# Two layers of long convolution and MLP on one core: another element order in the products with v, and the shift filter loaded once and copied on chip

## The chip, the core and the metric

The kernel runs on one core of one Trainium2 chip. Such a core has five engines, each with its own instruction stream: TensorE (PE; its weight loads are listed apart as PEld), VectorE (DVE), ScalarE (ACT), GpSimd (POOL) and SyncE (SP), which here only issues DMAs. Matmul results go to PSUM, from which DVE or ACT must fetch them; everything else lies in SBUF, 128 partitions wide. The metric is the device time of one execution in microseconds (us); the profile shows one execution, its times counted from the start of its span.

## The reference, cut to what matters

```python
def _A_ref(q, k, v, shift_k, ssm_k, ssm_D):            # B = 1, S = 2048, D = 512
    ks = shift_k.shape[-1]                             # 4 taps
    k_pad = jnp.pad(k, ((0, 0), (ks - 1, 0), (0, 0)))
    k_shift = jnp.zeros_like(k)
    for t in range(ks):
        k_shift = k_shift + k_pad[:, t:t + S, :] * shift_k[:, ks - 1 - t][None, None, :]
    kv = k_shift * v
    ...
    y = y + kv * ssm_D[None, None, :]                  # y: kv convolved with ssm_k over S, by FFT
    return q * y

def _B_ref(x, w1, b1, w2, b2):                         # F = 1376
    y = _layernorm(x, axis=-1)
    h = _gelu(jnp.einsum("bsd,df->bsf", y, w1) + b1)
    return jnp.einsum("bsf,fd->bsd", h, w2) + b2

x = A_q
x = x + _A_ref(_layernorm(x, axis=-1), A_k, A_v, A_shift_k, A_ssm_k, A_ssm_D)
x = x + _B_ref(_layernorm(x, axis=-1), B_w1, B_b1, B_w2, B_b2)
x = x + _A_ref(...)                                    # the same once more
x = x + _B_ref(...)
return x
```

All inputs and the output are bf16. The change touches `k_shift` (a filter of four taps over time, one for each channel) and `kv = k_shift * v`.

## The kernel before, in words

k, v and the filters are the same in both layers, so the long convolution `y` is computed once, in the first part of the program, and both layers use it. That part is a two-stage Fourier transform made of matmuls; the rest of the program, from some 96 us on, is nearly all MLP matmuls on PE.

The first part is not scheduled by a compiler. Each piece of work is an item with a name (`plan.add`), and the text table `ORDER` (line 19) lists all items with an engine letter: `kvm00.D` puts item kvm00 on DVE, `.A` is ACT, `.G` POOL, `.S` SP, and `.P2` is PE with PSUM buffer 2. Every engine runs its items strictly in the order of that table, and waits at an item until its inputs are there. There are four PSUM buffers, 4 KB a partition each, so two PSUM banks of 2 KB; an item that writes one waits until the last reader of that buffer is through.

The names that matter here:

- `lF, lK.., lk0, lk1, lW, lb1, lx0, lv0, lv1, lH`: loads issued by SP (line 279, the four of `ssm_k` line 342): a Fourier table, `ssm_k`, k, the table `Wt`, a bias, part of q, v in two halves, and a last table. They stand in one DMA queue.
- `lT0` to `lT3`: the shift filter, loaded four times (line 349), each time to 32 partitions. `taps_t` is a zeroed tile of 128 partitions x 16 groups x 7 columns, and load `lTi` puts the four taps of 16 channel groups into columns i to i+3 of partitions 32i to 32i+31. In memory a channel's four taps are 8 bytes, and in the tile they land 14 bytes apart, so each load is 512 pieces of 8 bytes.
- `dg0` to `dg3` (line 409, POOL): multiply the taps by a 32 x 32 identity, which gives banded matrices `DG`; they wait for all four `lT`.
- `kT0` to `kT3`: k transposed on PE and copied to SBUF.
- `kv00` to `kv31` (PE, lines 474 and 475): the shift as matmuls of transposed k with `DG`. Item `kv{cc}{o}` makes, for channels cc modulo 4 and half o of the token blocks, 1024 fp32 values a partition in one PSUM buffer.
- `kvm00` to `kvm31` (DVE, line 483): the products, in place in `uv`, which holds v as bf16, 16 token blocks x 512 channels a partition. There are eight; each waits for its `kv` and for its half of v.
- `U{cc}S{q}` (PE, line 303): the first Fourier stage of the products, evicted to the tiles `ZT` by ACT or DVE (lines 211 and 213); then `U..T` (transposes), `X` (line 507), `T` (products with the filter's spectrum, line 522), `V` (line 530) and so on.
- `kd` (lines 366 and 367, evicted at 211 and 213): four small corrections to the loaded `ssm_k`; each eviction writes 32 bf16 a partition, 64 elements apart in SBUF.
- `s00`, `s01`, `s02`: layer norm of a part of q on DVE, POOL and DVE; `sa`, `sb`: copies inside SBUF by DMA; `lM`: a 2 MB table that takes the place of transposed k and so waits for all `kv`.

In PSUM a product's buffer is ordered e (4), i (8 token blocks), c (32); in `uv` the same element lies at token block i, channel 16 c + 4 e + cc.

Of the kernel before, what the change touches and what calls it, by code (L numbers as in the profile page):

```python
# [103 lines left out]
def kernel(ctx: ExitStack, tc: tile.TileContext, A_q, A_k, A_v, A_shift_k, A_ssm_k, A_ssm_D,  # L104
                 B_x, B_w1, B_b1, B_w2, B_b2, out):
    nc = tc.nc
    P = 128
    _, S, D = A_q.shape
    F = B_w1.shape[1]
    KS = A_shift_k.shape[1]  # L110
# [54 lines left out]
    taps_t = const.tile([P, NG4, NU], BF16, name="taps_t")  # L165
# [108 lines left out]
    with tc.tile_pool(name="ps", bufs=1, space=bass.MemoryType.PSUM) as ps:  # L274
        pf = [ps.tile([P, 1024], F32, name=f"p{i}") for i in range(4)]
        plan = _Plan({"ps": 4, "xb": NXB, "zt": NZT})

        def load(name, dst, src, nbytes, deps=(), eng="S", rank=0):
            return plan.add(name, {eng: 400}, deps, lambda it: nc.sync.dma_start(dst, src), dma=("copy", nbytes), rank=rank)  # L279
# [16 lines left out]
        def first_stage(name, src, cs, dst, deps, xbar, edeps):  # L296
# [22 lines left out]
            for h in range(2):  # L319
# [9 lines left out]
                def mms(o, h=h):  # L329
# [8 lines left out]
        kd4 = k_d.rearrange(TOK, p=P)  # L338
# [17 lines left out]
        lW = load("lW", Wt[:], W_h.ap().bitcast(BF16), 2 ** 20)  # L356
        lH = load("lH", GPt[:], GP_h.ap().bitcast(BF16), 2 ** 16)
# [3 lines left out]
        for c in range(16):  # L361
# [8 lines left out]
            def mms(o, c=c):  # L370
                for m in range(8):
                    for r in range(2):
                        nc.tensor.matmul(o[64 * r:64 * r + 64, m, :], Kd[:, 8 * c + m, :], Ft[:, 256 + P * r:256 + P * r + P],  # L373
                                         start=True, stop=True)
            _, e = mm_evac(f"KS{c // 2}{c % 2}", KSC, [kd, lF], mms, [8, P],
                           lambda c=c: Zk.rearrange("p k (g m) -> p k g m", g=4)[:, :, :, 8 * c:8 * c + 8],
                           src=lambda v: v.rearrange("p m (g k) -> p k g m", g=4))
            KSe.append(e)
        KW, KX, KWp = [], [], []
        for j in range(NA // 2):  # L380
            def mms(o, j=j):
                for i in range(2):
                    nc.tensor.matmul(o[:, i, :], Wt[:, 2 * j + i, :], Zk[:, 2 * j + i, :], start=True, stop=True)
            pe, ev = mm_evac(f"K2{j}", K2C, [lW] + KSe, mms, [2, D], lambda j=j: ZK[:, :, 2 * j:2 * j + 2, :],
                             src=lambda v: v.rearrange("p k (t c) -> p t k c", t=CT))
# [14 lines left out]
        for i, (n, c) in enumerate(((13, 11), (1, 1), (1, 1))):  # L400
            it = plan.add(f"wm{i}", {"P": 427 * c}, [], warm, take=["ps"])
            it["n"] = n
            it["free"] = [(it, "ps")]
        kTp, kTe, dg = [], [], []
        DG = [view(xbb[NXB - CT + ct], [4, NU * 32]) for ct in range(CT)]
        for ct in range(CT):
            def diag(it, ct=ct):
                eng = nc.vector if it["eng"] == "D" else nc.gpsimd
                eng.tensor_tensor(DG[ct].rearrange("p g (u c) -> p g u c", c=32),
                                  apf(ID4, 0, [[32, P], [0, 4], [0, NU], [1, 32]]),  # L410
                                  apf(taps_t, ct * NU, [[NG4 * NU, P], [CT * NU, 4], [1, NU], [0, 32]]), ALU.mult)
            dg.append(plan.add(f"dg{ct}", {"D": 1000, "G": 2000}, lT, diag))
        for q in range(4):
            def mms(o, q=q):
                for g in range(NG4):
# [1 line left out]
            pe, ev = mm_evac(f"kT{q}", 1250, [lk[q // 2]], mms, [NG4, P], lambda q=q: kT[:, :, q, 2:2 + P], True)  # L417
# [9 lines left out]
        lx0 = load("lx0", lna0, xd[:, 0:GT, :], 2 ** 19)  # L427
# [39 lines left out]
        def taps(cc, o, deps):  # L467
            def mms(v):
                for e in range(4):
                    for b in range(2):  # L470
                        g, q = CT * e + cc, 2 * o + b
                        before = kT[:, g, q - 1, 2:2 + P] if q else kT[:, g, 3, 1:1 + P]
                        d = v[:, 2 * e + b, :]
                        nc.tensor.matmul(d, kT[:, g, q, 2:2 + P], DG[cc][:, e, 0:P], start=True, stop=False)
                        nc.tensor.matmul(d[:, 0:96], before, DG[cc][:, e, P:NU * 32], start=False, stop=True)  # L475
            pe = plan.add(f"kv{cc}{o}", {"P": 800}, deps + [dg[cc]],
                          lambda it: mms(view(pf[it["slot"]["ps"]], [8, P])), take=["ps"])
            kvp.append(pe)

            def mul(it):  # L480
                us = uv[:, 8 * o:8 * o + 8, :].rearrange("p i (c e x) -> p i c e x", e=4, x=4)[:, :, :, :, cc]
                ks = view(pf[pe["slot"]["ps"]], [4, 8, 32]).rearrange("p e i c -> p i c e")
                nc.vector.tensor_tensor(us, ks, us, ALU.mult)  # L483
            return plan.add(f"kvm{cc}{o}", {"D": 1150}, [pe, lv[o]], mul, free=[(pe, "ps")])
        um = [[taps(cc, o, [kTe[2 * o], kTe[2 * o + 1], kTe[2 * o - 1]]) for o in range(2)] for cc in range(CT)]
# [59 lines left out]
        w1 = load("w1", W1t[:], B_w1.rearrange("(ct p) f -> p ct f", p=P), 1376 << 10, Vps[0] + Vps[1])  # L545
# [284 lines left out]
```

## Time and profile before

| | |
|---|---|
| median of the timed runs (3) | 256.64 us, from 256.40 to 256.84 |
| the profiled execution | 255.45 us, of which the span is 253.6 us |
| mean granted TensorE clock | 0.991 |
| busy in the span: PE, DVE, ACT, POOL | 234.0, 178.3, 140.1, 37.6 us |
| DVE's products (line 483) | 32.7 to 51.3 us, 8 instructions |
| first MLP matmuls (line 662) | 95.7 us |

The profile's rows are read so. A row of a timeline has the start, the length, the engine, the line of the kernel, the operation, what it writes and reads, the shape a partition count x elements, and how many instructions were merged into the row; in brackets the idle time of the engine ahead of it and what ended that. A row of a group has the count, the busy time and the mean duration of one in ns, and behind the second bar the idle time ahead of such instructions. Names of tiles are those of the program; `arena` stands for several regions of one large tile (k, v, spectra and weights among them), `p` for the PSUM buffers. Durations of neighbours on an engine can overlap by some 0.1 to 0.2 us, since the next one starts while the last ends.

### The profile page before, as it was taken

How to read it: one execution, taken by the hardware profiler on the slowest of the kernel's cores; microseconds unless marked ns; L12 is line 12 of the kernel's file. 1: busy time of each engine (PE TensorE's matmuls, PEld its weight loads, DVE VectorE, ACT ScalarE, POOL GpSimd, SP SyncE). 2: the span in 40 equal slices, each digit the busy share in tenths (PEclk: the TensorE clock that was granted, in tenths of full speed). 3: DMA queues.
4: the chain of work that ended last, by engine and by line, in shares of the span. 5: the costliest groups of instructions: out<-in, count | busy, mean ns of one | idle time of the engine just before them, and what ended most of it. 6: DMA issues, size and time to landing. Idle time of an engine off the chain costs nothing.

```text
span 253.6 us, 4775 instructions
## 1 busy us (share of the span) xinstructions
PE 234.0 (92%) x1941; PEld 140.1 (55%) x1941; DVE 178.3 (70%) x316; ACT 140.1 (55%) x197; POOL 37.6 (15%) x49
## 2 busy tenths in 40 slices
PE   6967978789599899999999999999999999999994
PEld 2755657688498749744444444444444444444443
DVE  0585999989999989889889897866866862022022
ACT  2576975779679999933703713713713713713700
POOL 5000480016500031310111110110110110000000
PEclk9999997999999999999999999999999999999999
DMA  7999988299966999440510404004006006001001
GB/s 134 180 277 325 345 301 301 60 361 203 257 101 130 163 263 187 145 83 0 44 42 1 83 0 85 0 0 84 3 26 141 0 23 145 0 27 56 3 28 55
DMA packets 58129, 29.55 MB, mean 117 GB/s; under 512 B 50582, under 2 KB 54395, under 8 KB 57212
## 3 DMA queue, kind: packets, MB, share of 16 engines
q1 hardware_dynamic: 58100, 29.25, 48.3%
q8 instruction: 15, 0.25, 0.4%
q14 instruction: 6, 0.05, 0.1%
q10 hardware_dynamic: 8, 0.00, 0.0%
HBM read 15.10 MB, written 2.10 MB: 68 GB/s over the span
## 4 chain that ended last, share of the span: by engine, by line
PE 66%; DMA 12%; DVE 10%; SPq 5%; ACT 4%; issue 2%; DVEq 0%; ACTq 0%
PE po L752 30%; PE ph L718 26%; DMA arena<-in_A_v_dram 4%; DVE arena L483 4%; DMA arena<-arena 4%; PE p L662 4%; SPq L342 4%; DMA Wt<-tabW 3%; DVE arena L522 3%; PE p L530 2%; ACT ZT L211 2%; SPq L279 2%; PE p L507 1%; ACT xb L211 1%; ACT arena L211 1%
## 5 line engine op out<-in xcount | busy, mean ns | idle before, releaser
L720 ACT ACTIVATE arena<-ph,B 128x512 bf16<-128x512 f32 (+1 forms) x77 | 52.9, 687 | 78.4 <-PE ph L718 78.3
L752 PE MATMUL po<-arena 128*128 128x512 bf16 (+2 forms) x363 | 77.4, 372 | 0.0
L718 PE MATMUL ph<-arena 128*128 128x512 bf16 (+1 forms) x308 | 67.6, 379 | 0.0
L752 PEld LDWEIGHTS <-arena 128*128 128x128 bf16 (+1 forms) x363 | 35.4, 98 | 40.5
L757 DVE TENSOR_TENSOR arena<-po,arena 128x512 bf16<-128x512 f32 (+1 forms) x33 | 21.6, 673 | 46.4 <-PE po L752 46.4
L718 PEld LDWEIGHTS <-arena 128*128 128x128 bf16 (+1 forms) x308 | 30.8, 100 | 35.9
L211 ACT ACTIVATE arena<-p 128x1024 bf16<-128x1024 f32 (+7 forms) x45 | 39.8, 983 | 13.6 <-PE p L373 5.7
L211 ACT ACTIVATE ZT<-p 128x1024 bf16<-128x1024 f32 (+1 forms) x25 | 24.1, 1026 | 7.5 <-PE p L303 7.4
L213 DVE CAST arena<-p 128x1024 bf16<-128x1024 f32 (+1 forms) x13 | 13.2, 1077 | 11.1 <-PE p L367 9.0
L233 DVE BATCH_NORM_STATS2 lstm<-arena 128x6 f32<-128x512 bf16 x32 | 20.1, 681 | 0.3
L522 DVE TENSOR_TENSOR arena<-xb,arena 128x2048 bf16<-128x2048 bf16 (+1 forms) x15 | 20.1, 1404 | 0.0
L233 DVE BATCH_NORM_STATS2 lstg<-arena 128x6 f32<-128x512 bf16 x32 | 19.7, 677 | 0.0
L530 PE MATMUL p<-arena,arena 128*128 128x128 bf16 x256 | 16.2, 219 | 3.7 <-DVE arena L213 3.5
L483 DVE TENSOR_TENSOR arena<-p,arena 128x1024 bf16<-128x1024 f32 x8 | 18.6, 2502 | 0.4 <-PE p L475 0.4
L249 POOL TENSOR_TENSOR lrsm<-lrsm,mhalf 128x4 f32<-128x4 f32 (+2 forms) x11 | 9.9, 903 | 55.9 <-DVE lrsm L243 55.9
L249 POOL TENSOR_TENSOR lrsg<-lrsg,mhalf 128x4 f32<-128x4 f32 x8 | 8.1, 1016 | 65.9 <-DVE lrsg L246 65.8
L530 PEld LDWEIGHTS <-arena 128*128 128x128 bf16 x256 | 14.8, 98 | 4.7 <-DVE arena L522 3.4
L254 DVE TENSOR_SCALAR arena<-arena,lmvg,lrsg 128x512 bf16<-128x512 bf16 x32 | 11.0, 408 | 6.8 <-POOL lrsg L249 6.8
L211 ACT ACTIVATE xb<-p 128x1024 bf16<-128x1024 f32 x15 | 15.0, 1063 | 0.0
L254 DVE TENSOR_SCALAR arena<-arena,lmvm,lrsm 128x512 bf16<-128x512 bf16 x32 | 11.5, 415 | 2.4 <-POOL lrsm L249 2.4
L303 PE MATMUL p<-Ft,arena 128*128 128x256 bf16 x64 | 10.0, 291 | 3.1 <-DVE arena L483 3.0
L213 DVE COPY arena<-p 128x2048 bf16<-128x2048 bf16 x9 | 10.7, 1218 | 2.8 <-PE p L416 1.7
(69 smaller groups left out, 217.0 us busy)
## 6 DMA issues: line engine op xcount, KB each, us to landing
arena<-arena SPq DMA_DIRECT2D x8, 512.0 KB, 4.4
arena<-in_A_ssm_k_dram SPq DMA_DIRECT2D x4, 512.0 KB, 7.2
arena<-in_A_k_dram SPq DMA_DIRECT2D x2, 1024.0 KB, 9.6
arena<-in_A_v_dram SPq DMA_DIRECT2D x2, 1024.0 KB, 8.5
arena<-tabM SPq DMA_DIRECT2D x1, 2048.0 KB, 8.3
out_dram<-arena SPq DMA_DIRECT2D x15, 128.0 KB, 1.7
arena<-in_A_q_dram SPq DMA_DIRECT2D x1, 1536.0 KB, 7.0
arena<-in_B_w_dram SPq DMA_DIRECT2D x1, 1376.0 KB
```

The costliest lines, as they stand in the source:

```text
L211: nc.scalar.activation(dst, src, AF.Copy)
L213: nc.vector.tensor_copy(dst, src)
L233: nc.vector.bn_stats(self.st[:, i, 0, :], x_t[:, GT * g + i, :] if src is None else src[:, i, :])
L249: nc.gpsimd.tensor_tensor(self.rs[:, a:b], self.rs[:, a:b], mhalf[:, a:b], ALU.pow)
L254: eng.tensor_scalar(out=dst[:, i, :], in0=xs, scalar1=self.mv[:, i, 0:1], scalar2=self.rs[:, i:i + 1], op0=ALU.subtract, op1=ALU.mult)
L483: nc.vector.tensor_tensor(us, ks, us, ALU.mult)
L522: eng.tensor_tensor(kk, x2, kk, ALU.mult)
L530: nc.tensor.matmul(o[:, i, :], spec[:, cc, ka + i, :], Mt[:, ka + i, r, :], start=r == 0, stop=r == 1)
L718: nc.tensor.matmul(o.rearrange("p (i t) -> p i t", t=P), W1t[:, ct, ft * P:ft * P + m], lt[:, a:b, ct, :], start=ct == 0, stop=ct == CT - 1)
L720: nc.scalar.activation(hT[0:m, ft, a * P:b * P], o, AF.Gelu_apprx_tanh, bias=B1[0:m, ft:ft + 1])
L752: nc.tensor.matmul(po[:, a:b], hT[0:m, ft, i * P:(i + 1) * P], W2t[0:m, ft, a:b], start=ft == 0, stop=ft == FT - 1)
L757: nc.vector.tensor_tensor(xs, po[:, a:b], xs, ALU.add)
```

## The change

Two things are edited. First, the products walk their elements in another order: before, innermost e, then c, then i; now innermost c, then i, outermost e. PSUM is then read in a row, and in `uv` an element is followed by the one 16 channels on instead of the one 4 channels on. Which elements are multiplied does not change.

Second, the four loads of the shift filter become one, `lT`, which brings the filter four times to 32 partitions each, 128 bytes a partition, into a region `raw`; a new item `tb` on POOL, ahead of `dg0`, copies it to the four places in `taps_t`. The region `raw` lies where `sa1` and `sb1` write later. In the table, four words for loads go, `lT.S` comes between `lx0` and `lk1`, and `tb.G` ahead of `dg0.G`; nothing else moves in it.

```diff
 ORDER = """
...
-lx0.S lk1.S KS41e.A lT0.S kT1.P3
+lx0.S lT.S lk1.S KS41e.A kT1.P3
...
-KS21.P1 lT3.S KS71e.D
+KS21.P1 KS71e.D
...
-K26.P1 K210e.A dg0.G
+K26.P1 K210e.A tb.G dg0.G
...
 """
...
-        lT = [load(f"lT{i}", taps_t[32 * i:32 * i + 32, :, i:i + KS],
-                   apf(A_shift_k, 0, [[NG4 * KS, 32], [KS, NG4], [1, KS]]), 2 ** 13) for i in range(4)]
+        raw = place("raw", [P, NG4, KS], 82 * K)
+        lT = load("lT", raw, apf(A_shift_k, 0, [[0, 4], [NG4 * KS, 32], [1, NG4 * KS]]), 2 ** 14)
+
+        def band(it):
+            eng = nc.vector if it["eng"] == "D" else nc.gpsimd
+            for i in range(4):
+                eng.tensor_copy(taps_t[32 * i:32 * i + 32, :, i:i + KS], raw[32 * i:32 * i + 32, :, :])
+        tb = plan.add("tb", {"D": 400, "G": 600}, [lT], band)
...
-            dg.append(plan.add(f"dg{ct}", {"D": 1000, "G": 2000}, lT, diag))
+            dg.append(plan.add(f"dg{ct}", {"D": 1000, "G": 2000}, [tb], diag))
...
             def mul(it):
-                us = uv[:, 8 * o:8 * o + 8, :].rearrange("p i (c e x) -> p i c e x", e=4, x=4)[:, :, :, :, cc]
-                ks = view(pf[pe["slot"]["ps"]], [4, 8, 32]).rearrange("p e i c -> p i c e")
+                us = uv[:, 8 * o:8 * o + 8, :].rearrange("p i (c e x) -> p e i c x", e=4, x=4)[:, :, :, :, cc]
+                ks = view(pf[pe["slot"]["ps"]], [4, 8, 32])
                 nc.vector.tensor_tensor(us, ks, us, ALU.mult)
```

SP's queue in the first part of the program, from the table `Wt` to the last table, as one piece of the difference (`taps_t` is the banded tile, `in_A_shift_k_dram` the filter, `arena_67` holds a part of q here, `arena_65` k, `arena_66` v):

```order
 L279 DMA Wt<-tabW 128x4096
 L279 DMA arena_64<-in_B_b_dram 1x1376
-L279 DMA taps_t<-in_A_shift_k_dram 32x16x4 x2
 L279 DMA arena_67<-in_A_q_dram 128x2048
+L279 DMA arena_64<-in_A_shift_k_dram 128x1x64
 L279 DMA arena_65<-in_A_k_dram 128x4096
-L279 DMA taps_t<-in_A_shift_k_dram 32x16x4 x2
 L279 DMA arena_66<-in_A_v_dram 128x4096 x2
 L279 DMA GPt<-tabGP 128x256
```

Three DMAs fewer stand ahead of v, and the filter's one load stands ahead of the second half of k.

POOL from the program's preparations to the layer norm's scale (`ID_71` is the identity, `xb_105` to `xb_108` hold the banded matrices):

```order
 L185 COPY ID_71<-IDt 32x32 x4
 L190 COPY Dz<-arena_64 1x128 x3
-L409 TENSOR_TENSOR xb_105<-ID_71,taps_t 128x896
-L409 TENSOR_TENSOR xb_108<-ID_71,taps_t 128x896
-L409 TENSOR_TENSOR xb_107<-ID_71,taps_t 128x896
-L409 TENSOR_TENSOR xb_106<-ID_71,taps_t 128x896
+L355 COPY taps_t<-arena_64 32x16x4 x4
+L415 TENSOR_TENSOR xb_105<-ID_71,taps_t 128x896
+L415 TENSOR_TENSOR xb_108<-ID_71,taps_t 128x896
+L415 TENSOR_TENSOR xb_107<-ID_71,taps_t 128x896
+L415 TENSOR_TENSOR xb_106<-ID_71,taps_t 128x896
 L246 TENSOR_SCALAR lrsg_111<-lmvg_110 128x4
```

Four copies come ahead of the four diagonals, which only change their line.

DVE at the beginning of the products, before (`arena128_67` is transposed k, `arena112_66` is `uv`, `p0` to `p3` the PSUM buffers, in brackets the semaphores waited for):

```order
L213 COPY arena128_67<-p3_127 128x16x128 [waits PE_49,Activation_49]
L213 COPY arena128_67<-p2_126 128x16x128 [waits PE_49,Activation_49]
L483 TENSOR_TENSOR arena112_66<-p1_125,arena112_66 128x1024 [waits DMAHW7_49,PE_49,Activation_49]
L483 TENSOR_TENSOR arena112_66<-p0_124,arena112_66 128x1024 [waits PE_49,Activation_49]
L483 TENSOR_TENSOR arena112_66<-p1_125,arena112_66 128x1024 [waits DMAHW0_49,PE_49]
```

And with the change:

```order
L213 COPY arena128_67<-p3_127 128x16x128 [waits PE_49,Activation_49]
L213 COPY arena128_67<-p2_126 128x16x128 [waits PE_49,Activation_49]
L489 TENSOR_TENSOR arena112_66<-p1_125,arena112_66 128x4x256 [waits DMAHW4_49,PE_49,Activation_49]
L489 TENSOR_TENSOR arena112_66<-p0_124,arena112_66 128x4x256 [waits PE_49,Activation_49]
L489 TENSOR_TENSOR arena112_66<-p1_125,arena112_66 128x4x256 [waits DMAHW5_49,PE_49]
```

The products keep their places and buffers; the shape tells the new order, four runs of 256, and the loads of v signal through other semaphores.

More of the change, by code (lines that the diff above doesn't have):

```diff
@@ L18 @@
 ORDER = """
-lF.S lK11.S wm0.P3 lK00.S kd6.P0 kd6e.D KS70.P1 KS60.P2 KS70e.A lK01.S kd0.P3 KS61.P0 kd0e.D KS00.P3 KS61e.A KS60e.D KS11.P1 KS10.P2 KS11e.A KS01.P0 lK10.S lk0.S kd2.P1 KS00e.D kd2e.A lW.S KS71.P3 KS10e.D lb1.S KS01e.A KS21.P1 lT3.S KS71e.D KS21e.A KS20.P2 KS30.P0 kd4.P3 kd4e.A lT1.S KS31.P1 KS30e.A KS20e.D KS51.P3 KS40.P2 KS31e.D KS40e.A KS41.P0 KS51e.D KS50.P1 kT0.P2 lx0.S lk1.S KS41e.A lT0.S kT1.P3 kT0e.A KS50e.D K20.P0 K211.P1 K22.P2 K20e.A K22e.A kT1e.D K28.P3 K212.P0 K211e.D K28e.D K23.P1 K212e.A K214.P2 K215.P3 K214e.D K23e.A bB.P0 K29.P1 lT2.S lv0.S lv1.S bBe.D K215e.A K25.P2 K29e.A K210.P0 kT3.P3 K25e.A s00.D K26.P1 K210e.A dg0.G kT2.P2 K26e.A K27.P0 kT3e.D K27e.A K24.P3 dg3.G kv00.P1 kT2e.D lH.S K21.P2 K24e.A sb2.S kv30.P0 dg2.G K21e.A K213.P3 kvm00.D kv01.P1 U0S0.P20 kvm30.D K213e.A kv20.P0 U3S0.P31 kvm01.D U0S0e.A dg1.G s01.G kvm20.D U3S0e.A U0S2.P1 kv21.P2 U0S1.P0 sb1.S sa2.S kv11.P3 U0S2e.A U0S1e.A U2S0.P12 kvm21.D U2S0e.A U0S3.P2 U0S3e.A kv31.P0 kvm11.D U2S3.P3 kvm31.D kv10.P1 U2S2.P2 U2S3e.A U2S2e.A U2S1.P0 kvm10.D sb3.S s02.D U2S1e.A U0T0.P3 U3S1.P1 sb0.S U3S2.P2 U0T0e.D sa0.S U2T0.P0 U2T0e.D U3S1e.A U3S3.P1 X00.P30 U3S2e.A U3S3e.A X00e.A U0T1.P2 X20.P01 sa1.S U1S0.P10 U2T1.P3 U0T1e.D X20e.A X02.P22 lM.S U2T1e.D U1S2.P0 U1S0e.A X03.P13 sa3.S U1S3.P3 X02e.A X03e.A U1S1.P2 X21.P14 U1S2e.D U1S1e.A U1S3e.D U3T0.S X21e.A X22.P05 X23.P26 X01.P37 T00.G X22e.A T03.D X01e.A T02.D V00.P1 X23e.A U1T0.P0 ly.S V03.P3 V00e.A U3T1.S T20.D V02.P2 V03e.A T01.D U1T1.P1 U1T0e.D X30.P38 V01.P0 V02e.A U1T1e.D X11.P20 X30e.A X10.P13 T22.G V01e.A X12.P32 X11e.D T23.D V20.P02 X10e.A T21.D X13.P21 V22.P1 X12e.A X13e.A V22e.A V23.P3 T10.D V20e.A V21.P2 lx.S V23e.D X31.P17 Z01.S V21e.A Z00.S V10.P00 X33.P35 X32.P26 Z21.S T11.D X31e.A T12.D Z03.S V10e.A Z20.S X32e.A wm2.P1 V11.P1 V12.P0 T13.D T30.D V11e.A V13.P2 V12e.A V30.P11 T31.D V13e.A wm1.P0 X33e.A V30e.A T32.D Z23.S Z10.S T33b.D V31.P2 Z13.S V32.P0 T33a.D Z11.S V33b.P3 V33a.P1 w1.S V32e.D V31e.A V33be.A V33ae.A TD0a.P2 TD0b.P3 TD3.P0 TD0ae.A TD0be.A Y00.P1 LG1.D Z12.S TD3e.A Y00e.A TD1.P2 Y01.P3 g00.D q1.G Y32.P0 Y01e.A g01.D Z22.S h00.D TD1e.A Z02.S h01.D p00.G b00.D p01.G Y32e.A Y30.P1 Y02.P2 Y30e.A b01.D Y12.P3 Y10.P0 LT0.P1 Y02e.A g02.D Y12e.A TD2.P2 h02.D LT1.P3 LT0e.A p02.G w3.S a1.D w2.S TD2e.A LT1e.A M0a.P1 M0b.P2 M1b.P3 Y10e.A M0ae.A b02.D g10.D M1be.A M1a.P0 M0be.A LT2.P1 h10.D Y20.P3 LT2e.A Y22.P2 w4.S M2a.P1 g12.D Y20e.A M1ae.A M2c.P3 Y22e.A M2ce.A p10.G h12.D p12.G M2ae.A M2b.P0 b12.D b10.D M2be.A LT3.S
@@ new lines @@
+lF.S lK11.S wm0.P3 lK00.S kd6.P0 kd6e.D KS70.P1 KS60.P2 KS70e.A lK01.S kd0.P3 KS61.P0 kd0e.D KS00.P3 KS61e.A KS60e.D KS11.P1 KS10.P2 KS11e.A KS01.P0 lK10.S lk0.S kd2.P1 KS00e.D kd2e.A lW.S KS71.P3 KS10e.D lb1.S KS01e.A KS21.P1 KS71e.D KS21e.A KS20.P2 KS30.P0 kd4.P3 kd4e.A KS31.P1 KS30e.A KS20e.D KS51.P3 KS40.P2 KS31e.D KS40e.A KS41.P0 KS51e.D KS50.P1 kT0.P2 lx0.S lT.S lk1.S KS41e.A kT1.P3 kT0e.A KS50e.D K20.P0 K211.P1 K22.P2 K20e.A K22e.A kT1e.D K28.P3 K212.P0 K211e.D K28e.D K23.P1 K212e.A K214.P2 K215.P3 K214e.D K23e.A bB.P0 K29.P1 lv0.S lv1.S bBe.D K215e.A K25.P2 K29e.A K210.P0 kT3.P3 K25e.A s00.D K26.P1 K210e.A tb.G dg0.G kT2.P2 K26e.A K27.P0 kT3e.D K27e.A K24.P3 dg3.G kv00.P1 kT2e.D lH.S K21.P2 K24e.A sb2.S kv30.P0 dg2.G K21e.A K213.P3 kvm00.D kv01.P1 U0S0.P20 kvm30.D K213e.A kv20.P0 U3S0.P31 kvm01.D U0S0e.A dg1.G s01.G kvm20.D U3S0e.A U0S2.P1 kv21.P2 U0S1.P0 sb1.S sa2.S kv11.P3 U0S2e.A U0S1e.A U2S0.P12 kvm21.D U2S0e.A U0S3.P2 U0S3e.A kv31.P0 kvm11.D U2S3.P3 kvm31.D kv10.P1 U2S2.P2 U2S3e.A U2S2e.A U2S1.P0 kvm10.D sb3.S s02.D U2S1e.A U0T0.P3 U3S1.P1 sb0.S U3S2.P2 U0T0e.D sa0.S U2T0.P0 U2T0e.D U3S1e.A U3S3.P1 X00.P30 U3S2e.A U3S3e.A X00e.A U0T1.P2 X20.P01 sa1.S U1S0.P10 U2T1.P3 U0T1e.D X20e.A X02.P22 lM.S U2T1e.D U1S2.P0 U1S0e.A X03.P13 sa3.S U1S3.P3 X02e.A X03e.A U1S1.P2 X21.P14 U1S2e.D U1S1e.A U1S3e.D U3T0.S X21e.A X22.P05 X23.P26 X01.P37 T00.G X22e.A T03.D X01e.A T02.D V00.P1 X23e.A U1T0.P0 ly.S V03.P3 V00e.A U3T1.S T20.D V02.P2 V03e.A T01.D U1T1.P1 U1T0e.D X30.P38 V01.P0 V02e.A U1T1e.D X11.P20 X30e.A X10.P13 T22.G V01e.A X12.P32 X11e.D T23.D V20.P02 X10e.A T21.D X13.P21 V22.P1 X12e.A X13e.A V22e.A V23.P3 T10.D V20e.A V21.P2 lx.S V23e.D X31.P17 Z01.S V21e.A Z00.S V10.P00 X33.P35 X32.P26 Z21.S T11.D X31e.A T12.D Z03.S V10e.A Z20.S X32e.A wm2.P1 V11.P1 V12.P0 T13.D T30.D V11e.A V13.P2 V12e.A V30.P11 T31.D V13e.A wm1.P0 X33e.A V30e.A T32.D Z23.S Z10.S T33b.D V31.P2 Z13.S V32.P0 T33a.D Z11.S V33b.P3 V33a.P1 w1.S V32e.D V31e.A V33be.A V33ae.A TD0a.P2 TD0b.P3 TD3.P0 TD0ae.A TD0be.A Y00.P1 LG1.D Z12.S TD3e.A Y00e.A TD1.P2 Y01.P3 g00.D q1.G Y32.P0 Y01e.A g01.D Z22.S h00.D TD1e.A Z02.S h01.D p00.G b00.D p01.G Y32e.A Y30.P1 Y02.P2 Y30e.A b01.D Y12.P3 Y10.P0 LT0.P1 Y02e.A g02.D Y12e.A TD2.P2 h02.D LT1.P3 LT0e.A p02.G w3.S a1.D w2.S TD2e.A LT1e.A M0a.P1 M0b.P2 M1b.P3 Y10e.A M0ae.A b02.D g10.D M1be.A M1a.P0 M0be.A LT2.P1 h10.D Y20.P3 LT2e.A Y22.P2 w4.S M2a.P1 g12.D Y20e.A M1ae.A M2c.P3 Y22e.A M2ce.A p10.G h12.D p12.G M2ae.A M2b.P0 b12.D b10.D M2be.A LT3.S
```

## The prediction

> **What bounds the kernel now.** I read the windows first (a stretch, its length, then busy us of PE, its weight loads, DVE, ACT, POOL, the granted clock, the DMA share), to find the stage that the change lies in.
>
> ```profile
> 32.00:52.00 20.00, 15.08 (x188) 12.93 (x185) 19.59 (x12) 12.47 (x14) 5.32 (x7) 0.91 0.65 232
> 52.00:60.00 8.00, 7.81 (x114) 7.39 (x113) 6.92 (x8) 8.00 (x9) 4.07 (x1) 1.00 1.10 269
> 60.00:70.00 10.00, 6.61 (x114) 6.36 (x112) 10.00 (x7) 7.78 (x9) 4.34 (x1) 1.00 1.12 265
> 70.00:107.00 37.00, 35.48 (x474) 29.50 (x474) 34.53 (x64) 35.43 (x60) 4.67 (x6) 1.00 0.86 167
> ```
>
> From 32 to 52 us DVE is busy 19.59 of 20 us; PE has 4.9 us to spare and ACT 7.5. Over the whole span PE is the busiest engine, but not here. The timeline of DVE (start, length, instructions) says with what:
>
> ```profile
> 29.96 2.36 DVE L213 COPY arena<-p 128x2048 bf16<-128x2048 bf16 x2
> 32.73 18.58 DVE L483 TENSOR_TENSOR arena<-p,arena 128x1024 bf16<-128x1024 f32 x8 [0.41 <-PE p L475]
> 51.09 1.36 DVE L254 TENSOR_SCALAR arena<-arena,lmvg,lrsg 128x512 bf16<-128x512 bf16 x4
> 52.36 2.36 DVE L213 COPY arena<-p 128x2048 bf16<-128x2048 bf16 x2
> ```
>
> The eight products with v run back to back for 18.58 us. Who waited in that stretch, by groups of instructions:
>
> ```profile
> L474 PE MATMUL p<-xb,arena 128*128 128x128 bf16 x56 | 7.2, 234 | 1.9 <-DVE arena L483 1.9
> L303 PE MATMUL p<-Ft,arena 128*128 128x256 bf16 x37 | 6.4, 304 | 3.0 <-DVE arena L483 3.0
> L211 ACT ACTIVATE ZT<-p 128x1024 bf16<-128x1024 f32 x11 | 11.1, 1025 | 7.5 <-PE p L303 7.4
> 51.36 1.03 PE L303 MATMUL p<-Ft,arena 128*128 128x256 bf16 x8 [0.81 <-DVE arena L483]
> ```
>
> PE waits for products, ACT waits for PE, and at 51.36 PE goes on only when the last product is done (U3S1 writes the PSUM buffer that this product reads). The chain of waits agrees:
>
> ```profile
> 34.99 6.88 DVE arena L483 x3
> 44.19 2.52 DVE arena L483
> ```
>
> So what one product costs is worth eight times that, nearly whole, up and down. Up: behind the last product every engine's order follows it. Down: only until PE is the bound.
>
> **The change, part by part.**
>
> *The products.* The instruction walks the same 1024 elements in another order. Before, neighbours in time lie 8 bytes apart in uv (SBUF, read and written) and 1024 bytes apart in PSUM. After, they lie 4 bytes apart in PSUM, without gaps, and 32 bytes apart in uv. Which of the two sides makes a product dear now? Groups by form (count, busy us, mean ns):
>
> ```profile
> L483 DVE TENSOR_TENSOR arena<-p,arena 128x1024 bf16<-128x1024 f32 x8 | 18.6, 2502 | 0.4 <-PE p L475 0.4
> L213 DVE CAST ZT<-p 128x1024 bf16<-128x1024 f32 x4 | 4.8, 1218 | 0.0
> L213 DVE CAST xb<-p 128x1024 bf16<-128x1024 f32 x1 | 1.2, 1225 | 0.6 <-PE p L507 0.6
> L631 DVE TENSOR_TENSOR arena<-arena,p 128x512 bf16<-128x512 bf16 x2 | 1.4, 684 | 0.4 <-ACT arena L211 0.4
> L757 DVE TENSOR_TENSOR arena<-po,arena 128x512 bf16<-128x512 f32 x31 | 20.7, 689 | 45.1 <-PE po L752 45.1
> L757 DVE TENSOR_TENSOR arena<-po,arena 128x256 bf16<-128x256 f32 x2 | 0.8, 425 | 1.3 <-PE po L752 1.3
> ```
>
> The casts into ZT read PSUM in steps of 1024 bytes, four at a time, as the products do (`p i (j k) -> p k j i` with i innermost), and write runs of four bf16 in SBUF. They take 1218 ns, the cast into xb, which reads PSUM in a row, 1225. L631 is a product that reads PSUM in steps of 512 bytes, with SBUF in a row: 684 ns, against 689 for L757 with everything in a row. So PSUM out of a row costs nothing in a cast nor in a product, and what is left of the 2502 ns is the step in SBUF. That step becomes four times as wide.
>
> For single bf16 elements at a wider step there is one place in the trace, the evictions `kd`, which write 32 elements 128 bytes apart in SBUF from PSUM in a row:
>
> ```profile
> L213 DVE CAST arena<-p 128x32 bf16<-128x32 f32 x2 | 0.6, 301 | 9.0 <-PE p L367 9.0
> L213 DVE COPY B<-p 128x11 f32<-128x11 f32 x1 | 0.2, 159 | 0.0
> L211 ACT ACTIVATE arena<-p 128x32 bf16<-128x32 f32 x2 | 0.6, 317 | 1.7 <-PE p L367 1.7
> L211 ACT ACTIVATE arena<-p 128x512 bf16<-128x512 bf16 x2 | 1.2, 600 | 0.0
> L211 ACT ACTIVATE arena<-p 128x256 bf16<-128x256 bf16 x1 | 0.4, 384 | 0.4 <-PE p L564 0.4
> ```
>
> DVE's fixed part is 161 ns by L757 (689 for 512, 425 for 256: 1.03 ns an element) or at most 148 by the copy of 11 (159 less 11 x 1.04). The 301 ns then leave 4.4 to 4.8 ns for each of the 32. ACT: 600 for 512 and 384 for 256 give 0.84 ns an element and 168 fixed; (317 - 168) / 32 = 4.7 ns. Two engines, one price. Now the products: 18.58 / 8 = 2.32 us each, 2.27 ns an element. At 8 bytes two of them share each 16 bytes of SBUF, so that a 16-byte piece costs 4.54 ns: the price of one kd element, alone in its piece. **The value I take** is therefore a price by the piece: at 32 bytes every element has a piece to itself and costs 4.54 ns. 1024 x 4.54 = 4.65 us a product, 2.33 more than now; **eight are +18.6 us**. With 4.4 ns it is +17.5, with 4.8 +20.7. The other end is a product at the cast's price, 1.22 us; it stands among the rivals. All of the 18.6 is on the path: PE, ACT and the loads behind the last product only start later. The 1.1 us in which DVE waits between 52 and 60 might be won back at most; I take none, since PE stands still at U3S1 in the same way.
>
> [...]
>
> *The filter's loads.* Four loads of 512 pieces of 8 bytes go, one load and four copies on POOL come, each 32 x 64. On SP, POOL and the waits:
>
> ```profile
> 14.92 1.92 SPq L279 DMA_DIRECT2D taps_t<-in_A_shift_k_dram  x2
> 19.15 2.17 SPq L279 DMA_DIRECT2D taps_t<-in_A_shift_k_dram  x2
> 22.57 1.73 SPq L279 DMA_DIRECT2D arena<-in_A_v_dram  x2
> 28.93 6.66 POOL L409 TENSOR_TENSOR xb<-ID,taps_t 128x896 bf16<-128x896 bf16 x4 [23.79 <-DMA taps_t<-in_A_shift_k_dram]
> L185 POOL COPY ID<-IDt 32x32 bf16<-32x32 bf16 x4 | 0.8, 204 | 0.1
> L190 POOL COPY Dz<-arena 1x128 bf16<-1x128 bf16 x4 | 1.2, 288 | 1.1 <-DMA arena<-in_A_ssm_D_dram 1.0
> PEld L416 <- DMA arena<-in_A_k_dram: 1.5, 2, 1.2
> 23.24 12.11 ACT L211 ACTIVATE arena<-p 128x1024 bf16<-128x1024 f32 x13 [0.94 <-PE p L383]
> ```
>
> SP issues some 4 us less, and the loads of q, k and v start earlier. v is not waited for: in the DVE row above the first product waits 0.41 us, for PE. The only wait for a load behind the filter's is the second one for k, 1.5 - 1.2 = 0.3 us. The first products are held by ACT, which evicts 13 tiles without a gap from 23.24 on; that run starts with the table Wt, ahead of the filter in the queue. So at best 0.4 us are won. Behind the new load the four copies cost 0.8 to 1.2 us on POOL (204 to 288 ns each) ahead of the four diagonals L409; of those the first is through at 30.6, and the first product's matmuls start at 31.7. The load is issued before the second part of k instead of after it, so POOL starts earlier than 28.93; if it did not, the second diagonal would be late by 0.8 us at most. Range -0.4 to +0.8 us; I take 0. The wait of one SP load (into the region that holds the raw filter) for POOL's copies ends before that load's other waits.
>
> *Sum.* The profiled execution takes 255.45 us (span 253.6); with +18.6 it is 274.1. The median of the timed runs is 256.64, 1.2 us above that execution, so I forecast **275.2 us** for the median.
>
> **The rivals.**
>
> *The price in SBUF does not depend on the step* (the change then does nothing to the products). For it: only two widths are in the trace, 8 and 128 bytes, and kd's 32 elements are few; a fixed part 70 ns larger would bring its price down to 2.27 ns. Against it: ACT's kd shows the same price with its own fixed part. A product stays at 2.32 us, give or take 0.1: 256.6, from 255.4 (-0.8 and -0.4) to 258.2 (+0.8 and +0.8). [...]
>
> *PSUM is the dear side after all* (or SBUF is dear because neighbours fall into one piece), and the products fall to the cast's 1.22 us. For it: no row shows a product that reads two PSUM banks out of a row. Against it: the ZT casts do just that at full speed. DVE would save 8 x 1.1 = 9 us, but PE waited for products only 1.9 + 3.0 = 4.9 us, and then PE's 15.1 us of work bind: 256.6 - 4.9 = **251.7**; with ACT's whole 7.5 us of waiting 249.1. This is the faster side; it decides as soon as a product is below 2.3 us. [...]
>
> [...]
>
> **How the numbers follow.** Price by the piece 0.50 (273 to 278: +17.5 less 1.1, to +20.7 and 0.8); price unchanged 0.20, of which faster 0.05, same 0.09, slower 0.06; in between 0.05; products at the cast's price 0.23; dearer than 4.8 ns 0.02. Faster by over 0.2% 0.28, within 0.2% (0.5 us, about what a measurement of this kernel can tell from no change) 0.09, slower 0.63. The range goes from 251.0, which takes in more than half of the faster case, to 279.0.
>
> **What would show it.** The group of the products, now at L489: near 4.8 us is the forecast, 2.5 the first rival, 1.2 the second. PE's wait for products in the window from 32 us on: near 20 us if they double, near nothing if they halve. POOL's diagonals should start before 28.9, and no PE wait for them appear. The stretch from the last product to the end should keep its 202 us (253.6 - 51.3) whatever happens ahead of it. The forecast is wrong if single bf16 elements 32 bytes apart are not written one piece at a time, which no row of before shows.

## The result and the profile after

| | before | after |
|---|---|---|
| median of the timed runs | 256.52 us (4) | 273.36 us (4, from 272.99 to 274.74) |
| ratio of the times, 95% interval | | 1.0669, 1.0627 to 1.0711 |
| profiled execution, span | 255.45, 253.6 us | 272.99, 271.1 us |
| one product with v, mean | 2502 ns | 4663 ns |
| last product ends | 51.3 us | 67.0 us |

The change makes the kernel 6.7% slower, by 16.8 us. The forecast was 275.2 us, 18.6 more than before.

The timeline of DVE after the change (start, length, instructions), with the group of the products behind it:

```profile
29.45 2.35 DVE L213 COPY arena<-p 128x2048 bf16<-128x2048 bf16 x2
32.21 34.77 DVE L489 TENSOR_TENSOR arena<-p,arena 128x1024 bf16<-128x1024 f32 x8 [0.41 <-PE p L481]
66.59 1.46 DVE L254 TENSOR_SCALAR arena<-arena,lmvg,lrsg 128x512 bf16<-128x512 bf16 x4
67.95 2.37 DVE L213 COPY arena<-p 128x2048 bf16<-128x2048 bf16 x2
L489 DVE TENSOR_TENSOR arena<-p,arena 128x1024 bf16<-128x1024 f32 x8 | 34.8, 4663 | 0.4 <-PE p L481 0.4
```

The eight products take 34.77 us instead of 18.58, again without a gap: 4.35 us from one to the next, where it was 2.32 (the mean of 4663 ns counts the overlap with the next one, too). They begin 0.52 us earlier. Everything behind them begins 15.5 us later (66.59 against 51.09). The waits from 18 to 90 us (engine, what, on what: total, times, longest) show who paid:

```profile
ACT ZT L211 <- PE p L303: 23.6, 10, 4.4
PE p L303 <- DVE arena L489: 10.2, 6, 2.8
PE p L480 <- DVE arena L489: 5.9, 2, 3.0
```

PE waited 4.9 us for products before and 16.1 now, ACT for PE 7.4 before and 23.6 now. The forecast had near 20 us for PE; its matmuls themselves got slower, as two windows of the product stage show (the granted clock is third from the end of a row):

```profile
32.00:52.00 20.00, 10.55 (x104) 8.40 (x102) 19.79 (x5) 6.92 (x8) 1.05 (x3) 0.65 0.47 176
52.00:70.00 18.00, 11.36 (x113) 9.66 (x111) 18.00 (x10) 7.46 (x8) 0.00 (x0) 0.73 0.41 146
```

From 40 to 60 us the clock is 0.50, and from the first product to the last PE is busy 18.7 us instead of 13.7. This costs nothing here, since DVE still waits for nobody. The filter's part, on POOL and SP:

```profile
23.33 1.08 POOL L355 COPY taps_t<-arena 32x64 bf16<-32x64 bf16 x4 [18.23 <-DMA arena<-in_A_shift_k_dram]
24.50 6.65 POOL L415 TENSOR_TENSOR xb<-ID,taps_t 128x896 bf16<-128x896 bf16 x4
16.43 0.94 SPq L279 DMA_DIRECT2D arena<-in_A_v_dram  x2
```

The diagonals begin at 24.5 us instead of 28.9, the loads of v are issued at 16.4 instead of 22.6. Neither is waited for.

Behind the products one thing differs. PE's timeline there, first before and then after, and two windows of the same place after:

```profile
70.10 1.05 PE L530 MATMUL p<-arena,arena 128*128 128x128 bf16 x16 [3.50 <-DVE arena L213]
70.99 1.50 PE L507 MATMUL p<-arena,Wt 128*128 128x128 bf16 x24
85.73 1.86 PE L536 MATMUL p<-arena,arena 128*128 128x128 bf16 x16 [3.50 <-DVE arena L213]
87.39 2.36 PE L513 MATMUL p<-arena,Wt 128*128 128x128 bf16 x24
86.00:88.00 2.00, 2.00 (x21) 2.00 (x20) 0.81 (x1) 0.37 (x1) 0.00 (x0) 0.50 0.00 0
90.00:92.00 2.00, 2.00 (x40) 2.00 (x38) 2.00 (x3) 2.00 (x3) 0.00 (x0) 1.00 1.60 190
```

The same sixteen and twenty-four matmuls took 1.05 and 1.50 us before. Here the clock is 0.50 for 3.4 us behind a pause of PE of 3.5 us, a pause that is there before, too. That costs 1.6 us: from the first of these groups to the idle matmul that follows (line 399 before, 405 now) it is 10.18 us (85.73 to 95.91) against 8.58 (70.10 to 78.68). Together: +16.2 for the products, -0.5 for their start, +1.6 for the clock, +0.2 elsewhere, which is the 17.5 us between the two spans.

### The profile page after: what moved, and what is told of

Same layout as the page of the kernel before. It is cut to its first block, busy times and chain, and to the rows that moved or that the text cites. A ratio compares the mean times of both kernels' runs of the same rounds, so it can differ in the third digit from the quotient of the medians.

```text
span 271.1 us, 4773 instructions
## 1 busy us (share of the span) xinstructions
PE 240.4 (89%) x1941; PEld 145.3 (54%) x1941; DVE 194.5 (72%) x316; ACT 140.2 (52%) x197; POOL 38.6 (14%) x53
## 4 chain that ended last, share of the span: by engine, by line
PE 64%; DVE 15%; DMA 5%; SPq 5%; ACT 5%; issue 5%; DVEq 0%; ACTq 0%
PE po L758 28%; PE ph L724 25%; DVE arena L489 10%; PE p L668 4%; ACT ZT L211 3%; SPq L342 3%; DMA Wt<-tabW 3%; DVE arena L528 3%; PE p L536 2%; DMA arena<-ZT 2%; PE p L389 2%; SPq L279 2%; PE p L513 1%; DVE arena L213 1%; PE p L422 1%
## 5 line engine op out<-in xcount | busy, mean ns | idle before, releaser
L763 DVE TENSOR_TENSOR arena<-po,arena 128x512 bf16<-128x512 f32 (+1 forms) x33 | 21.6, 673 | 46.4 <-PE po L758 46.4
L211 ACT ACTIVATE ZT<-p 128x1024 bf16<-128x1024 f32 (+1 forms) x25 | 24.2, 1036 | 23.6 <-PE p L303 23.6
L489 DVE TENSOR_TENSOR arena<-p,arena 128x1024 bf16<-128x1024 f32 x8 | 34.8, 4663 | 0.4 <-PE p L481 0.4
L303 PE MATMUL p<-Ft,arena 128*128 128x256 bf16 x64 | 12.3, 334 | 10.2 <-DVE arena L489 10.2
L536 PEld LDWEIGHTS <-arena 128*128 128x128 bf16 x256 | 15.5, 100 | 4.5 <-DVE arena L528 2.7
L480 PE MATMUL p<-xb,arena 128*128 128x128 bf16 x64 | 10.8, 274 | 5.9 <-DVE arena L489 5.9
L303 PEld LDWEIGHTS <-arena 128*128 128x128 bf16 x64 | 7.5, 127 | 12.7 <-issue 9.3
```

The costliest lines, as they stand in the source:

```text
L211: nc.scalar.activation(dst, src, AF.Copy)
L303: nc.tensor.matmul(o[:, i, :], src[:, 4 * q + i, cs], Ft[:, 0:256], start=True, stop=True)
L536: nc.tensor.matmul(o[:, i, :], spec[:, cc, ka + i, :], Mt[:, ka + i, r, :], start=r == 0, stop=r == 1)
L763: nc.vector.tensor_tensor(xs, po[:, a:b], xs, ALU.add)
```

## The experiments

Theory: a single bf16 write into SBUF is priced by the 16-byte piece that it falls into, and the order in PSUM is free. Rivals: PSUM out of a row is the dear side; the price follows the hop, or reads have as large a part in it as writes. Each kernel is the one before with the edit shown, unless said otherwise; "a product" is the mean of its group by form.

**e1, the filter's part alone** (line 489 is then the old product).

> The kernel before with the filter's one load and four copies alone; products in the old order. Theory: the load part starts the products some 0.5 us earlier (32.21 us in the profile of the changed kernel against 32.73) and moves nothing else: 0.2 to 0.8 us faster than before, the product group at 2.50 us each. Rival: the copies on POOL and the other order of loads cost as much as they save: no difference.

Measured: 256.86 us (12 runs) against 257.21 (17 runs), ratio 0.9996, 0.996 to 1.0031: no difference.

```profile
L489 DVE TENSOR_TENSOR arena<-p,arena 128x1024 bf16<-128x1024 f32 x8 | 18.7, 2494 | 0.7 <-PE p L481 0.7
69.53 1.75 PE L536 MATMUL p<-arena,arena 128*128 128x128 bf16 x16 [3.49 <-DVE arena L213]
```

The products began at 31.71 us, 1.0 earlier than in the profile of before, but the slow stretch on PE is there as well and cost 1.6 us (10.14 us from line 536 to the idle matmul, against 8.58). If the filter's part gains its half microsecond, these runs do not show it.

**e2, PSUM in a row, SBUF as before.** PE writes the shifted k with its four e side by side:

```diff
-                        d = v[:, 2 * e + b, :]
+                        d = v[:, b, :, e]            # v: [2, P, 4]
...
-                ks = view(pf[pe["slot"]["ps"]], [4, 8, 32]).rearrange("p e i c -> p i c e")
+                ks = view(pf[pe["slot"]["ps"]], [8, 32, 4])
```

> The kernel before, but PE writes the shifted k so that its four channels e lie next to each other in PSUM: the products read PSUM in a row and step 8 bytes in SBUF as before. If PSUM out of a row is the dear side, a product falls from 2.50 to about 1.2 us and the kernel gets some 5 us faster. If the step in SBUF is the dear side, a product stays at 2.4 to 2.6 us; PE's writes 16 bytes apart may cost a little on PE.

```profile
L483 DVE TENSOR_TENSOR arena<-p,arena 128x1024 bf16<-128x1024 f32 x8 | 18.9, 2481 | 1.2 <-ACT arena L211 1.2
L474 PE MATMUL p<-xb,arena 128*128 128x128 bf16 x64 | 12.9, 308 | 0.4 <-DVE arena L483 0.4
```

2481 ns with PSUM in a row, 2502 without: DVE's order in PSUM is not what makes these products dear. Time 257.69 us in one run. PE's writes 16 bytes apart do cost: the matmul of line 474 goes from 232 to 308 ns, and in a group of 16 one begins every 0.1 us instead of every 0.05, at a granted clock of 1.00 in both.

**e3, written in a row.** The products go to the region where k lay, the first stage reads them there; v is read in 8-byte steps and PSUM out of a row as before:

```diff
+    u2 = place("u2", [P, CT, NT, P], 96 * K)
...
-                nc.vector.tensor_tensor(us, ks, us, ALU.mult)
+                nc.vector.tensor_tensor(u2[:, cc, 8 * o:8 * o + 8, :].rearrange("p i (c e) -> p i c e", e=4), ks, us, ALU.mult)
...
-            sp, zu = first_stage(f"U{cc}", uv, slice(cc, D, CT), chunk(ZX, cc), ...
+            sp, zu = first_stage(f"U{cc}", u2[:, cc, :, :], slice(0, P), chunk(ZX, cc), ...
```

> The kernel before, but the products are written in a row to the region where k lay, and the first stage reads them there; v is read in steps of 8 bytes and PSUM out of a row as before. If the price is that of single bf16 writes in SBUF, a product falls from 2.50 to about 1.2 us and the kernel gets 5 to 7 us faster, PE's or ACT's work being next. If the reads of v cost as much as the writes, a product stays at 2.3 to 2.5 us and the time with it. If PSUM's order is the dear side, likewise 2.5 us.

Measured: 250.28 us (6 runs) against 257.21, ratio 0.9702, 0.9653 to 0.9752.

```profile
L484 DVE TENSOR_TENSOR arena<-p,arena 128x1024 bf16<-128x1024 f32 x8 | 9.7, 1224 | 1.4 <-PE p L476 1.4
38.11 2.45 DVE L484 TENSOR_TENSOR arena<-p,arena 128x1024 bf16<-128x1024 f32 x2 [0.51 <-PE p L476]
41.00 2.45 DVE L484 TENSOR_TENSOR arena<-p,arena 128x1024 bf16<-128x1024 f32 x2 [0.44 <-PE p L476]
36.82 10.46 ACT L212 ACTIVATE ZT<-p 128x1024 bf16<-128x1024 f32 x11 [0.20 <-PE p L304]
```

A product is 1224 ns, what a cast of its size takes, though it reads PSUM in steps of 1024 bytes and v in steps of 8. So the whole excess was the write, and PSUM out of a row is free. The products are also no longer in place here; line 757, which is in place and in a row, takes 689 ns for 512 elements, and e8 below is dear without being in place, so that is not the cause. DVE now waits for PE between products, and ACT evicts without a gap: they are the next bound, as the rival with products at the cast's price had it, with 6.9 us between the medians instead of 4.9.

**e4, the products' new order alone**, with the four old loads.

> The kernel before with the products' new order alone, the four filter loads as before. Theory: a product near 4.66 us, the first starting near 32.7 us, and the kernel 16 to 18 us slower than before, 0.3 to 0.6 more than the whole change. Rival: part of the 4.66 us comes from loads that now run beside the products at other times, and a product is clearly cheaper here.

```profile
L483 DVE TENSOR_TENSOR arena<-p,arena 128x1024 bf16<-128x1024 f32 x8 | 34.7, 4654 | 0.4 <-PE p L475 0.4
34.67 34.75 DVE L483 TENSOR_TENSOR arena<-p,arena 128x1024 bf16<-128x1024 f32 x8 [0.41 <-PE p L475]
```

4654 ns: the order alone makes the price. The one run took 276.81 us, 19.6 above the median of before and more than expected. Its mean granted clock was 0.938, against 0.948 in the profile of the change. In front, DVE waited for PE's matmuls of line 383 up to 2.7 us at once, where it was 1.0 before, and the first product came 1.9 us late (34.67). From the last product to the end it was 205.4 us, 3.1 more than before, with slow matmuls from 70 to 74 us (line 331, sixteen in 1.63 us at 70.34 against 1.06 at 75.53) and again behind PE's pause (line 507, twenty-four in 2.34 us against 1.50 before).

**e5 and e6, two instructions a product, in pairs.** Both take the same elements in the same number of instructions, two channels at a time: in e5 the two are 8 bytes apart, in one 16-byte piece, in e6 16 bytes apart, in two.

```diff
-                us = ....rearrange("p i (c e x) -> p i c e x", e=4, x=4)[:, :, :, :, cc]
+                for h in range(2):
+                    us = ....rearrange("p i (c f e x) -> p i c f e x", f=2, e=2, x=4)[:, :, :, h, :, cc]     # e5
+                    us = ....rearrange("p i (c f e x) -> p i c f e x", f=2, e=2, x=4)[:, :, :, :, h, cc]     # e6
```

> The kernel before, each product split into two instructions of 512 elements, by channels e in (0,1) and then (2,3): in time two writes 8 bytes apart, then a hop of 24 bytes on average (32 from pair to pair). If writes are priced by the 16-byte piece, each piece takes two in a row as before and one instruction costs 512 x 2.27 ns and its fixed part, some 1.25 us: no more than now for the pair. If the price follows the hop, it lies between 8 and 32 bytes: some 1.7 us each.

> The same split by e in (0,2) and then (1,3): in time two writes 16 bytes apart, then a hop of 16 bytes to the next pair, every write in another 16-byte piece. If writes are priced by the 16-byte piece, one instruction costs 512 x 4.25 ns and its fixed part, some 2.25 us, twice the other split. If the piece were 32 bytes, or the hop decided, it is 1.3 to 1.7 us.

```profile
32.82 18.20 DVE L484 TENSOR_TENSOR arena<-p,arena 128x512 bf16<-128x512 f32 x16 [0.41 <-PE p L475]
32.62 36.70 DVE L484 TENSOR_TENSOR arena<-p,arena 128x512 bf16<-128x512 f32 x16 [0.41 <-PE p L475]
```

The upper row is e5, the lower e6: 18.20 / 16 = 1.14 us an instruction against 2.29. Pairs that hop to the next 32 bytes cost what steps of 8 do, 2.22 ns a write against 2.27, where both fall into one 16-byte piece; 16 bytes apart a write cost 4.48 ns. The mean hop is 16 bytes in both, so the hop does not decide, nor a piece of 32 bytes. One run each: 256.43 and 276.41 us.

**e7 and e8, the read and the write apart.** e7 reads v in steps of 32 bytes and writes in a row; e8 writes in steps of 32 bytes and reads in a row, elements of k in place of v. Neither computes the reference: e7 leaves the channels in another order, and e8 leaves v out.

```diff
+                dst = u2[:, cc, 8 * o:8 * o + 8, :].rearrange("p i (e c) -> p e i c", e=4)          # e7
+                nc.vector.tensor_tensor(dst, ks, us, ALU.mult)
...
+                vs = kn[:, 8 * o:8 * o + 8, :].rearrange("p i (x e c) -> p x e i c", e=4, x=4)[:, cc]   # e8
+                nc.vector.tensor_tensor(us, ks, vs, ALU.mult)
```

> The products read v in steps of 32 bytes and PSUM in a row, and write in a row to the region where k lay (channels of a quarter come out in another order, so the transform's filter meets the wrong channels). If reads are free at any step, a product is 1.2 us, as with v read in steps of 8. If a read has the same price by the piece as a write, it is 4.3 to 4.7 us; a price between shows a read price of its own, hidden at 8 bytes.

> The products as changed, PSUM in a row and written in steps of 32 bytes, but multiplied with elements of k that lie in a row in place of v. If writes alone make the price, a product stays at 4.5 to 4.7 us and the time near 275 us. If the read of v at 32 bytes has a part in it, a product is clearly below 4.5 us.

```profile
32.94 15.54 DVE L485 TENSOR_TENSOR arena<-p,arena 128x1024 bf16<-128x1024 f32 x8 [0.41 <-PE p L476]
L484 DVE TENSOR_TENSOR arena<-p,arena 128x1024 bf16<-128x1024 f32 x8 | 34.9, 4674 | 0.4 <-PE p L475 0.4
```

e8 is the changed kernel's price (4674 against 4663 ns): the write makes it alone. e7 is a price between: 15.54 / 8 = 1.94 us a product, 1.9 ns an element, where reads 8 bytes apart had cost nothing in e3. So reads at this step pay too, but less, and behind the write they are hidden; whether they also pay by the piece no run shows. One run each: 254.85 and 274.84 us.

**e9, token blocks innermost**, writes 1024 bytes apart.

> The kernel before with token blocks innermost: in time the writes lie 1024 bytes apart in SBUF, the reads of PSUM 128 bytes. If a lone write has one price whatever the hop, a product costs what it does at 32 bytes, 4.5 to 4.7 us. [...]

```profile
32.67 35.68 DVE L483 TENSOR_TENSOR arena<-p,arena 128x1024 bf16<-128x1024 f32 x8 [0.41 <-PE p L475]
```

35.68 / 8 = 4.46 us, against 4.35 at 32 bytes: nearly one price for a lone write at these two hops. One run: 275.74 us.

**e10, idle matmuls in PE's pause, on the changed kernel.** The table gets `wm3.P2` between `X30` and `V01`. The expectation has it that nobody uses their results; in fact they are written over one tile of the transform's last stage (`V02`) before it is fetched, so this kernel leaves that tile out of its result.

> The changed kernel with twelve matmuls of 512 columns, whose results nobody uses, on PE right ahead of the matmuls that wait 3.5 us at 85.7 us in its profile and then run at 1.86 us for 16 and 2.36 for 24 instead of 1.05 and 1.50 us before. If PE's pause there makes the clock fall, these come back to 1.05 and 1.50 us, and the kernel gains about 1.6 us. If the clock falls for the idle time of the whole product stage or for another reason, the slow stretch stays.

```profile
87.63 1.05 PE L536 MATMUL p<-arena,arena 128*128 128x128 bf16 x16 [0.91 <-DVE arena L213]
67.23 1.86 PE L303 MATMUL p<-Ft,arena 128*128 128x256 bf16 x8 [1.65 <-DVE arena L489]
```

The groups behind the pause are at a clock of 1.00 (86 to 92 us), but the time of the one run is the same, 273.29 us: in this execution the clock was 0.50 right behind the products instead, from 66 to 70 us (1.86 us for what took 1.03 at the same place in the profile of the change).

**e11, the best of both**: the filter's part and the products of e3.

> The filter in one load and four copies, the products in the old order but written in a row to the region where k lay. Theory: the two gains add: a product 1.22 us, the first one near 32.2 us, 6 to 8 us faster than before. Rival: with the products short, PE waits at the front for the diagonals or for v, and the filter's part gives more or less than its 0.5 us.

Measured: 249.20 us (6 runs, 248.39 to 251.16) against 257.79, ratio 0.9686, 0.964 to 0.9731. A product is 1224 ns; the first one began at 32.84 us, so nothing of the filter's half microsecond is to be seen, and the interval overlaps that of e3. In this execution the matmuls that wait for `Wt` began at 22.72 us, 0.6 later than in the profile of the change, and the first product came later by as much.

**e12, e11 with ten idle matmuls** in the pause, with the tile `V02` fetched first (`X30.P38 V02e.A wm3.P2 V01.P0`).

> The best version so far (products written in a row, filter in one load) with ten matmuls of 512 columns, whose results nobody uses, in PE's 3.8 us pause ahead of the group of 16 matmuls that took 1.05 us in its own profile and 1.87 us in that of the version with the old loads. If that pause is what lets the clock fall in some executions, the group is 1.05 us here too and the median falls by up to 1.6 us below 249.2, with less spread. If the fall has another cause, median and spread stay within 0.5 us.

Measured: 248.09 us (6 runs, 247.81 to 249.20) against 257.75, ratio 0.9636, 0.96 to 0.9671.

```profile
59.92 2.32 PE L406 MATMUL p<-IDt 128*128 128x512 bf16 x10 [0.31 <-ACT arena L212]
63.49 1.05 PE L537 MATMUL p<-arena,arena 128*128 128x128 bf16 x16 [1.26 <-DVE arena L214]
```

Median and spread fall as expected of the pause, by 1.1 us and from 2.8 to 1.4. But the two intervals overlap, and the two profiled executions, in both of which the clock is 1.00 behind the pause (62 to 68 us), are alike (spans of 247.2 and 247.3 us): a gain over e11 is possible and not shown. Against both kernels of the case this is the fastest.

## Why the prediction was right

- **The stage and the engine.** The products bound the stretch from 32 us on, up as well as down: 16.2 us more of products made the rest 15.5 to 15.7 us later, the difference being the earlier start.
- **PSUM is free, SBUF is dear.** Read from the casts into ZT and from L631. e3 shows both directly: 1224 ns with PSUM out of a row and only the write in SBUF put in a row.
- **The price by the 16-byte piece.** Worked out from two rows, the products' 2.27 ns at two to a piece and kd's 4.4 to 4.8 ns at one. e5 and e6 show the piece, e8 that the write sets the price and e9 that the hop hardly does.
- **The size of that term.** 4.54 ns an element was taken, 4.25 measured (34.77 us / 8 / 1024), 4.36 at 1024 bytes, 4.48 at 16. Twice the price of a pair is a little more than a lone write at 32 bytes. So the term was +18.6 and measured +16.2. That the forecast of the time was off by only 1.8 us is partly luck: the clock, which the working had at nothing, gave 1.6 us back in the profile.
- **The filter's part.** Taken at 0, from -0.4 to +0.8: the products started 0.5 us earlier in the profile, and e1 cannot tell the whole from nothing. The reason given for at most 0.4 us, the second wait for k, was not what moved. In 12 of the 14 profiles (not e2 and e4) the first product begins 10.1 to 10.3 us after the matmuls that wait for `Wt`, and those began at 22.09 us instead of 22.60, though `Wt` stands ahead of the filter in the queue. They began between 22.1 and 23.1 us in the nine profiles with the old loads and between 21.6 and 22.8 in the five with the new, so an earlier `Wt` through the filter's load is not shown.
- **What was missing.** The stretch from the last product to the end was to stay at 202 us; it was 204.1 (271.1 - 67.0), through the clock of 0.50 behind PE's pause. It was not to depend on what happens ahead of it, but with the dear products it does: in five of the six profiles that have them (e4, e6, e8, e9, e10, not that of the change) PE's matmuls were slow right behind the last product as well: the first sixteen of line 331 took 1.63 to 1.91 us there, against 1.06 with the change, and in e10 the windows give a clock of 0.50. From there to the matmuls behind the pause it was 20.4 to 21.6 us in these, against 18.8 in the profiles of before and of the change. And the profile of before, which the working leans on, was an execution with the clock at 1.00 from 52 to 92 us; that is likely a part of the 1.2 us between it and the median, which no second profile of it shows.
- **The rivals.** "Unchanged", "in between" (2.7 to 4 us a product) and "dearer than 4.8 ns" fell with 4663 ns. "Cast's price" had its size right and its side wrong: a product does fall to 1.22 us, but when the write is in a row, not the read of PSUM, and it gave 6.9 us (e3), more than the 4.9 by PE's waits and near the 7.5 by ACT's.

## What to carry to other kernels

Where DVE scatters single bf16 elements, count how many writes in a row fall into one 16-byte piece of SBUF (here 4.25 to 4.5 ns a write alone in its piece, 2.2 to 2.3 by two), and write in a row into a free region if there is one (here 1.2 ns); the reading side forgave more (1.9 ns at 32 bytes, e7), and PSUM's order was free for DVE here (2481 ns in a row, 2502 without). Before an access order is turned around for one operand, look for the other groups in the same profile that already use either order: here two casts and a tiny eviction told which operand was dear and what the new order would cost. That kd's price came out alike on DVE and ACT (4.4 to 4.8 and 4.7 ns) pointed to the memory and not to the engine; the experiments changed writes of DVE alone.

Look at the granted clock by windows before a stretch is called unchanged: here PE's wait for products grew from 4.9 to 16.1 us, its clock in that stage fell from 0.91 to 0.66, and in five of the six profiles with the dear products PE's matmuls were slow into the next stage (1.63 to 1.91 us for sixteen that took 1.06).

## What the runs showed of the hardware

Lone bf16 writes into SBUF by DVE: 4.25 to 4.5 ns each in a piece of their own, 2.2 to 2.3 ns when two follow each other in one 16-byte piece, about 1.2 ns in a row. Reads of v beside writes in a row: nothing more at steps of 8 bytes, 1.9 ns an element at 32. PE's matmuls that write PSUM 16 bytes apart begin every 0.1 us instead of every 0.05 (e2).

Behind PE's pause of 3.5 to 3.8 us, ahead of line 530, PE's matmuls were slow in 9 of the 12 profiled executions without matmuls in that pause (not in the profile of before, nor in e6 and e11), and in none of the 2 with them (e10 and e12). Read by windows, the granted clock there was 0.50 for 3.4 us in the profile of the change and for 6.8 us in e3, and 1.00 in the profile of before, in e10, e11 and e12. In the other seven of the nine the matmuls alone tell it: the twenty-four of line 507 of the kernel before took 2.03 to 2.77 us, against 1.50 where the clock was 1.00. From the matmuls behind the pause to the next idle matmul the fall cost 1.3 to 1.6 us in eight of the nine and 2.6 in e3, and it is likely a part of the spread from run to run. In the product stage of the changed kernel, where PE is busy 63% of the time from 40 to 60 us, the clock stayed at 0.50 all through. What sets the clock no run shows: the slow stretch came and went between executions of nearly the same program. Since it stays away in some executions without the idle matmuls, two are too few to show that these keep it away.
